# A Fourier filter with a mixture of experts: transform pieces put behind expert steps at an even course, gate and lists in a bank and buffers of their own, float16 from the fourth set on

## The chip, the cores and the metric

The kernel runs on one core of a Trainium2 chip. The metric is device time in microseconds (us), the median over runs. Engines are named as the profile names them: PE (matmuls), PEld (its weight loads), DVE (vector), ACT (scalar), POOL (GpSimd) and SP, which issues most DMAs.

## What is computed

Eight batches of 2496 x 256 numbers are filtered along their length by a Fourier transform, a product and the inverse transform. The 19968 rows that come out go through a mixture of eight experts with noisy top-2 gating:

```python
X = np.fft.rfft(x, axis=1); y = np.fft.irfft(X * F[None], n=S, axis=1).reshape(B * S, D)
noisy = y @ w_gate + np.log1p(np.exp(y @ w_noise)) * noise
top2 = the two largest of each row; w = softmax over them
out[row] += w * (np.maximum(y[row] @ w1[e], 0) @ w2[e])    # for both experts e of the row
```

D is 256, the hidden width F is 1024.

## The kernel before

**Transform.** `fft_stream` writes the filter as a stream of small pieces: `s1` and `kg0` to `kg2` go to the frequencies and multiply, `t3` and `i2` come back, all as matmuls with small tables. Every operand is a sum of a high and a low part, so most products are three matmuls. The first two batches are transformed before any expert runs (`early`); the others stand between expert steps. A batch has two halves of 128 columns, `n` = 0 to 15. When its second half is back, `logit_sum`, `logits` and `gate` choose the experts, `slots` deals out blocks, and `route` makes the lists of rows: one-hot matrices `oc` on DVE, matmuls into `ra` on PE, an indirect add on POOL.

**Experts.** Once a batch is listed, a new *set* of blocks of 512 rows can run: 2, 12, 18, 24, 34, 44, 54, 64 blocks in total after each of the eight sets, then remainders. `expert` yields 13 steps per block: eight for the first product (`hps`, six matmuls of 128x512 each), one, and four for the second (`yps`, 24 matmuls of 128x256 each). ACT applies the relu (`hh`, line 1371), DVE makes the low part (`hl`, line 1372). `_mm3` (lines 123 to 126) writes the three matmuls, so its lines stand for both products and the tiles tell them apart. From set `HALF` on the operands are float16, scaled by powers of two that `wscales` finds (all weights are squared on ACT, `wp`, and the first batches of y are read back); before it they are 32-bit.

**Order.** `run` alternates the two: after each expert step it advances the stream while `PACE` allows, a number of transform steps per set, spread over the set. `pin` keeps rows in the written order on chosen engines; what is not pinned a scheduler orders by its own estimate, and expert steps and transform pieces mix freely there. `self.after(i)` keeps what follows behind instruction `i` on its engine.

**PSUM.** Eight banks: `hps` 2, `yps` 2, `xps` 1, `fps` 3. An expert's third bank is `xps` (line 1353); everything of transform, gate and lists shares `fps`:

```python
tag = self.banks.get(nm, "fps") if self.early else "fps"
third = ("xps", 1) if self.by_dma(ent) else ("yps", 2)
while (state["ready"] < state["i"] + (2 if state["i"] < ALONE else 1)
       and (state["n"] - state["p0"]) * state["len"] <= state["c"] * PACE.get(state["i"], PACES) and step()):
```

Of the kernel before, what the change touches and what calls it, by code (L numbers as in the profile page):

```python
# [24 lines left out]
NG = 22  # L25
# [97 lines left out]
def _mm3(nc, o, lh, ll, rh, rl, start=True, stop=True):  # L123
    nc.tensor.matmul(o, lh, rh, start=start, stop=False)  # L124
    nc.tensor.matmul(o, lh, rl, start=False, stop=False)  # L125
    nc.tensor.matmul(o, ll, rh, start=False, stop=stop)  # L126
# [6 lines left out]
PACE = {0: 110, 1: 200, 2: 60}  # L133
PACES = 115
FILL = {0: 0, 1: 14}
RAW = 3
HALF = 5
# [9 lines left out]
EARLY = {"q1": "hps", "q2": "hps", "q5": "yps", "q6": "yps", "u1": "xps", "u3": "yps"}  # L147
BANKS = {"hps": 2, "yps": 2, "xps": 1, "fps": 3}

MOVES = {0: {"q3": "yps"}, 12: {"q3": "fps"}, 14: {"q3": "yps", "q4": "yps", "q5": "hps", "q6": "hps"}, 26: {"q4": "fps", "q5": "yps", "q6": "yps"}}  # L150


class Moe:
# [40 lines left out]
    def setup(self):  # L194
# [43 lines left out]
        self.xs, self.scaled, self.known, self.owed, self.relu = {}, False, False, [], None  # L238

# [163 lines left out]
    def kg1(self, n, kg):  # L403
# [32 lines left out]
        self.zz[n, kg] = a  # L436

# [85 lines left out]
    def i2(self, n, g0):  # L523
# [12 lines left out]
        w = 128 + E * h  # L536
# [11 lines left out]
        if h:  # L548
            nc.scalar.copy(yt[:, :k, 128:], self.dense[:, g0:g0 + k])
# [122 lines left out]
    def fft_stream(self):  # L672
# [132 lines left out]
        for n in range(2 * FIRSTS, N + 1):  # L805
# [31 lines left out]
            for t in range(tot):  # L837
                while ix < len(X) and ix * tot <= t * len(X):
                    self.pin(X[ix], hold=self.held, only=self.held and [self.nc.tensor.engine])
                    ix += 1  # L840
                    write()
                    yield min(self.done_routes, self.rows)
                while iy < len(Y) and iy * tot <= t * len(Y):
                    if self.held:
                        self.pin(Y[iy], only=[self.nc.tensor.engine])
                    else:
                        Y[iy]()
# [11 lines left out]
    def gate(self, bt, lgp):  # L859
# [12 lines left out]
        nc.scalar.activation(u, lg[:, :, 8:16], AF.Exp)  # L872

# [11 lines left out]
        v.tensor_add(nz, l, lg[:, :, 0:8])  # L885
# [6 lines left out]
        for i in range(2):  # L892
            mi, ci = t(f"m{i}", [RP, NG]), t(f"c{i}", [RP, NG])
# [30 lines left out]
        v.tensor_add(self.dense, self.dense, nz)  # L924
        yield None
# [4 lines left out]

# [6 lines left out]
        v.scalar_tensor_tensor(rw, mm, float(LR - 1), q[:, 8:16], op0=ALU.add, op1=ALU.add)  # L937
# [8 lines left out]
        rb = t("rb", [RP, E])  # L946
        v.tensor_add(rb, q[:RP, 0:8], mm[:RP])
# [23 lines left out]
        v.tensor_add(self.base, self.base, q[:, 8:16])  # L971
        v.tensor_add(self.cnt, self.cnt, q[:E, 16:17])
# [60 lines left out]
    def route(self, bt, hi, lo, row, rf):  # L1033
# [11 lines left out]
        for g0 in range(0, NG, 4):  # L1045
            q = self.ps("ra")[:, :HR]
            for g in range(g0, min(g0 + 4, NG), 2):
                t = P.tile([128, 1024], F16, name="oc", tag=("xh", "xl", "b")[g // 2 % 3], bufs=1)


                ol, vv = t[:RP, 0:4 * LR], t[:RP, 4 * LR:4 * LR + 4 * HR]
                if bt < 2:
                    ol, vv = (a.rearrange("p (l j) -> p l j", j=4) for a in (ol, vv))
                else:
                    ol, vv = (a.rearrange("p (j l) -> p l j", j=4) for a in (ol, vv))

                def w(a):
                    return a if bt < 2 else a.rearrange("p l j -> p j l")

                v.tensor_tensor(w(vv), w(lr[:, :HR]), w(bc(hi[:, g:g + 2], HR)), op=ALU.is_equal)  # L1060
                v.tensor_mul(w(vv), w(vv), w(tv[:, 2 * g:2 * g + 4].unsqueeze(1).to_broadcast([RP, HR, 4])))
                v.tensor_tensor(w(ol), w(lr), w(bc(lo[:, g:g + 2], LR)), op=ALU.is_equal)
                for j in range(4):
                    n = RP if g + j // 2 < NG - 1 else QA
                    nc.tensor.matmul(q, ol[:n, :, j], vv[:n, :, j], start=(g == g0 and j == 0), stop=(j == 3 and g + 2 >= min(g0 + 4, NG)))
# [10 lines left out]
        o = P.tile([HR, LR], F32, name="ro", **(dict(tag="th", bufs=3) if bt < 2 else dict(tag="ut1", bufs=1)))  # L1076
# [257 lines left out]
    def expert(self, parts, may, fill=None):  # L1334
# [5 lines left out]
        while self.ahead:  # L1340
# [12 lines left out]
            third = ("xps", 1) if self.by_dma(ent) else ("yps", 2)  # L1353
            hh = []
            for f in range(8):
# [3 lines left out]
                for kc in range(2):  # L1359
                    wh, wl = w1[f // 2]  # L1360
                    o = (f % 2) * 128
                    _mm3(nc, p, wh[:, kc, o:o + 128], wl[:, kc, o:o + 128], *xT[kc], start=(kc == 0), stop=(kc == 1))
# [24 lines left out]
            for t in range(nt):  # L1387
# [5 lines left out]
                for f in range(8):  # L1393
                    h, l = (a[:, t * 128:(t + 1) * 128] for a in hh[f])
                    hl = w2[f // 2][:, :, f % 2]
                    _mm3(nc, p, h, l, hl[:, 0], hl[:, 1], start=(f == 0), stop=(f == 7))
# [11 lines left out]
    def run(self):  # L1408
# [58 lines left out]
        for _ in self.expert(parts(), may, fill):  # L1467
# [59 lines left out]
```

## Time and profile before

| | us |
|---|---|
| median of 3 runs | 2166.99 |
| lowest, highest run | 2159.28, 2168.4 |
| the profiled execution | 2164.38 |
| its span in the profile | 2162.5 |

Busy times of PE are unions of overlapping matmuls: each is shown with its time through the array, so the distance from one start to the next, not the shown duration, is what one costs. Idle time is shown in brackets behind a row with the engine and tile that ended it. A timeline merges equal neighbours (x4).

### The profile page before, as it was taken

The page shows a single profiled execution, that of the slowest core. Times are in us where ns is not written, and L with a number is a line of the kernel's source. Part 1 is how long each engine was busy: PE and PEld are TensorE (multiplying, and loading weights), DVE is VectorE, ACT ScalarE, POOL GpSimd, SP SyncE. Part 2 cuts the span into 40 slices and gives each one's busy share as a digit, 9 for nine tenths or more (in the row PEclk, how much of TensorE's full clock was granted, in tenths as well). Part 3 has the DMA queues.
Part 4 walks back from the last instruction along what each step waited for, and adds up shares of the span by engine and source line. Part 5 has one row for each costly group of instructions (what it writes and reads, how often), then busy time and mean ns, then how long its engine had stood idle before and what let it go on. Part 6 is the DMA issues. An engine that isn't in the chain of part 4 may idle for free. (4 is left out here: it accounts for less than half of the span.)

```text
span 2162.5 us, 42794 instructions
## 1 busy us (share of the span) xinstructions
PE 2095.9 (97%) x14517; PEld 1595.5 (74%) x14517; DVE 1466.3 (68%) x3221; ACT 1286.1 (59%) x2505; POOL 1029.2 (48%) x946
## 2 busy tenths in 40 slices
PE   8779999999999999999999999999999999999997
PEld 6447988888888888766766676666666666667886
DVE  5866779877978886678665986589666664333443
ACT  6666866786577446656664565555566564333443
POOL 4233334434544344445444453555655665654563
PEclk9989999999999999999999999999999999999999
DMA  9588989999999775767766687666889999869997
GB/s 255 165 259 223 222 223 215 252 228 228 223 214 233 161 156 137 178 150 183 155 156 131 152 182 165 146 121 132 233 210 240 240 249 234 170 142 229 276 280 175
DMA packets 511673, 428.48 MB, mean 198 GB/s; under 512 B 215679, under 2 KB 397015, under 8 KB 511447
## 3 DMA queue, kind: packets, MB, share of 16 engines
q1 hardware_dynamic: 450135, 341.27, 60.2%
q0 software_dynamic: 61312, 84.40, 23.1%
q8 instruction: 116, 1.90, 0.4%
q14 instruction: 110, 0.90, 0.1%
HBM read 263.92 MB, written 122.03 MB: 178 GB/s over the span
## 5 line engine op out<-in xcount | busy, mean ns | idle before, releaser
L1372 DVE SCALAR_TENSOR_TENSOR hl<-hps,hh 128x512 f16<-128x512 f32 (+3 forms) x712 | 432.4, 623 | 356.6 <-ACT hh L1371 354.7
L1399 POOL DMA_INDIRECT out<-stage,ids x316 | 532.9, 1686 | 270.4 <-ACT stage L1398 167.0
L1158 POOL DMA_INDIRECT stage<-y,ids x316 | 347.9, 1101 | 535.7 <-DMA xt<-stage 433.9
L124 PE MATMUL yps<-w,hh 128*128 128x256 f16 (+1 forms) x2048 | 556.5, 278 | 5.2 <-ACT stage L1398 3.4
L125 PE MATMUL yps<-w,hh 128*128 128x256 f16 (+1 forms) x2048 | 551.2, 277 | 0.0
L126 PE MATMUL yps<-w,hl 128*128 128x256 f16 (+1 forms) x2048 | 541.9, 277 | 1.8 <-DVE hl L1372 1.5
L1371 ACT ACTIVATE hh<-hps 128x512 f16<-128x512 f32 (+3 forms) x712 | 376.7, 550 | 198.9 <-PE hps L126 183.8
L125 PE MATMUL hps<-mxl,w1h 128*128 128x512 f16 (+1 forms) x1024 | 394.4, 386 | 2.2 <-DVE mxl L1246 1.3
L126 PE MATMUL hps<-mxh,w1l 128*128 128x512 f16 (+1 forms) x1024 | 394.0, 386 | 0.0
L124 PE MATMUL hps<-mxh,w1h 128*128 128x512 f16 (+1 forms) x1024 | 385.6, 388 | 5.1 <-DVE hl L1372 5.1
L1398 ACT ACTIVATE stage<-yps,gt 128x256 f32<-128x256 f32 x316 | 143.1, 475 | 329.0 <-PE yps L126 202.0
L124 PEld LDWEIGHTS <-hh 128*128 128x128 f16 x1760 | 172.2, 98 | 52.4 <-issue 6.2
L126 PEld LDWEIGHTS <-hl 128*128 128x128 f16 x1760 | 171.5, 98 | 47.9 <-DVE hl L1372 1.9
L125 PEld LDWEIGHTS <-hh 128*128 128x128 f16 x1760 | 172.2, 98 | 34.2 <-issue 2.6
L124 PEld LDWEIGHTS yps<-w,hh 128*128 128x128 f32 x768 | 145.8, 190 | 12.5 <-ACT stage L1398 2.2
L126 PEld LDWEIGHTS yps<-w,hl 128*128 128x128 f32 x768 | 145.0, 190 | 10.3 <-issue 1.7
L125 PEld LDWEIGHTS yps<-w,hh 128*128 128x128 f32 x768 | 145.4, 191 | 4.6
L126 PEld LDWEIGHTS <-w1l 128*128 128x128 f16 x640 | 62.6, 98 | 71.8 <-issue 1.5
L541 ACT COPY yt<-q 117x1024 uint16<-117x1024 uint16 x96 | 90.9, 947 | 40.7 <-PE q L535 32.1
L1228 DVE COPY stage<-xt 128x1024 uint16<-128x1024 uint16 (+2 forms) x174 | 109.0, 679 | 1.4 <-DMA xt<-stage 1.4
L124 PEld LDWEIGHTS <-w1h 128*128 128x128 f16 x640 | 62.4, 98 | 51.5 <-issue 5.5
L125 PEld LDWEIGHTS <-w1h 128*128 128x128 f16 x640 | 62.6, 98 | 51.1 <-issue 3.0
(286 smaller groups left out, 4024.4 us busy)
## 6 DMA issues: line engine op xcount, KB each, us to landing
stage<-w SPq DMA_DIRECT2D x328, 256.0 KB
x<-x SPq DMA_DIRECT2D x88, 256.0 KB
fd<-c SPq DMA_DIRECT2D x77, 240.0 KB
fi<-wpl SPq DMA_DIRECT2D x18, 1024.0 KB
fx<-fd SPq DMA_DIRECT2D x140, 128.0 KB
out<-z SPq DMA_DIRECT2D x24, 702.0 KB
wp<-w SPq DMA_DIRECT2D x64, 256.0 KB
fr<-w SPq DMA_DIRECT2D x16, 1024.0 KB
```

Of the source, the lines that this page charges most:

```text
L124: nc.tensor.matmul(o, lh, rh, start=start, stop=False)
L125: nc.tensor.matmul(o, lh, rl, start=False, stop=False)
L126: nc.tensor.matmul(o, ll, rh, start=False, stop=stop)
L541: e = nc.scalar.copy(yt.bitcast(U16)[:, :k, :256].rearrange("p g (two d) -> p g two d", two=2), p.bitcast(U16)[:RP, :2 * m].rearrange("p ( ...
L1158: self.pin(lambda: nc.gpsimd.indirect_dma_start(out=x.bitcast(I32), out_offset=None, in_=self.y[:BLK + ready * ROWS], in_offset=bass.Indir ...
L1228: nc.vector.tensor_copy(xu.rearrange("p (t two) -> p two t", two=2), ent[3][0][:, 2 * kc:2 * kc + 2, :w])
L1371: self.relu = hold(lambda: nc.scalar.activation(h, p, AF.Relu))
L1372: v = hold(lambda: nc.vector.scalar_tensor_tensor(l, p, 0.0, hf[0], op0=ALU.max, op1=ALU.subtract))
L1398: nc.scalar.activation(o, p, AF.Copy, scale=gate[:, t])
L1399: a = nc.gpsimd.indirect_dma_start(out=self.io["out"][:BLK + ready * ROWS], out_offset=bass.IndirectOffsetOnAxis(ap=ids[:, t:t + 1], axis= ...
```

## The change

1. Pieces of the transform on PE stand behind the last matmul that an expert wrote (`self.mm`), and those on ACT behind the last relu.
2. `COURSE` replaces `PACE`: a line through points (expert steps, transform steps), and the stream may always be one set further ahead.
3. `HALF` goes from 5 to 4: the fourth set runs in float16, its scales are due by step 202 (`READY`) instead of 280.
4. Gate, slots and lists (`APART`) use the bank `xps`; the experts' third bank is `yps` until all lists are done. For batches from the third on, what is read from that bank is copied out (`clean`, `total`, `below`).
5. `route` builds the one-hots of up to two groups (`place`), yields, and then multiplies (`add`); its buffers are `ut0`, `ul`, `ut1` and `gl`.
6. The chosen weights `dense` go to memory in one store per batch in place of a copy into each `yt`.
7. The planes of the tail are prepared from the last filter piece on (`filtered`), not from the last list on.

```diff
-PACE = {0: 110, 1: 200, 2: 60}
-PACES = 115
+COURSE = (0, 55), (100, 172), (178, 268), (256, 365), (386, 462), (516, 554), (646, 640)
-HALF = 5
+HALF = 4
+APART = {"lg", "rk", "sl", "st", "ra"}
+def due(y):
+    for (a, m), (b, n) in zip(COURSE, COURSE[1:]):
+        if y <= b:
+            return m + (n - m) * (y - a) / (b - a)
+    return float("inf")
...
-        tag = self.banks.get(nm, "fps") if self.early else "fps"
+        tag = self.banks.get(nm, "fps") if self.early else "xps" if nm in APART else "fps"
...
+        self.filtered = (n, kg) == (2 * NB - 1, 4)
...
-        w = 128 + E * h
+        w = 128 + (E * h if n < 4 else 0)
-        if h:
+        if h and n < 4:
             nc.scalar.copy(yt[:, :k, 128:], self.dense[:, g0:g0 + k])
...
-                    self.pin(X[ix], hold=self.held, only=self.held and [self.nc.tensor.engine])
+                    with self.after(self.mm), self.after(self.relu):
+                        self.pin(X[ix], hold=self.held, only=self.held and [self.nc.tensor.engine])
...
+        clean = lg[:, :, 0:8]
+        if bt >= 2:
+            clean = P.tile(sh, F32, name="clean", tag="oh1", bufs=1)
+            nc.scalar.copy(clean, lg[:, :, 0:8])
-        v.tensor_add(nz, l, lg[:, :, 0:8])
+        v.tensor_add(nz, l, clean)
...
+        if bt >= 2:
+            y = self.y[BLK + bt * ROWS:BLK + (bt + 1) * ROWS].rearrange("(p g) d -> p g d", p=RP)
+            nc.sync.dma_start(y[:, :, D:], self.dense.bitcast(I32))
...
+            below, total = t("rb", [RP, E]), P.tile([128, E], F32, name="total", tag="gd", bufs=1)
+            v.tensor_copy(total, q[:, 8:16])
+            v.tensor_copy(below, q[:RP, 0:8])
+            v.tensor_add(self.cnt, self.cnt, q[:E, 16:17])
...
+                t = P.tile([128, 4 * LR + 4 * HR], F16, name="oc", tag=("ut0", "ul", "ut1")[made % 3], bufs=1)
...
+                hot = [place(g) for g in gs]
+                yield
+                q = self.ps("ra")[:, :HR]
+                for g, o in zip(gs, hot):
+                    add(q, g0, g, *o)
...
-            third = ("xps", 1) if self.by_dma(ent) else ("yps", 2)
+            third = ("xps", 1) if self.done_routes == NB - 1 else ("yps", 2)
...
-            while (state["ready"] < state["i"] + (2 if state["i"] < ALONE else 1)
-                   and (state["n"] - state["p0"]) * state["len"] <= state["c"] * PACE.get(state["i"], PACES) and step()):
+            while (state["ready"] < state["i"] + 2
+                   and state["n"] <= due(state["y"]) and step()):
-            if state["ready"] >= NB - 1:
+            if self.filtered:
                 state["k"] += 1
```

Two places show how it moves instructions. The first is DVE where it builds the one-hots of the fifth batch's list (lines 1060 to 1062 before, 1089 to 1091 now; 1372 and 1417 are `hl`, 1323 and 1249 a weight split, 546 and 555 the maximum of y). Before:

```order
L1062 TENSOR_TENSOR oc<-half,lo 117x512
L1323 TENSOR_TENSOR w_10592<-stage,w_10592 128x512
L1067 COPY rx<-ra 128x56
L1060 TENSOR_TENSOR oc<-half,hi 117x224
L1062 TENSOR_TENSOR oc<-half,lo 117x512
L1060 TENSOR_TENSOR oc<-half,hi 117x224
L1062 TENSOR_TENSOR oc<-half,lo 117x512
L1323 TENSOR_TENSOR w_10617<-stage,w_10617 128x512
L546 TENSOR_REDUCE ymax<-yt 117x1
L400 TENSOR_TENSOR tl<-fx,th 128x512
L1372 SCALAR_TENSOR_TENSOR hl<-hps,hh 128x512
L1061 TENSOR_TENSOR oc<-oc,half 117x224
```

and now:

```order
L350 TENSOR_TENSOR xl<-x,xh 117x512
L1112 COPY rx<-ra 128x56
L1089 TENSOR_TENSOR oc<-half,hi 117x224
L1091 TENSOR_TENSOR oc<-half,lo 117x512
L438 TENSOR_TENSOR a<-a,b 128x512
L555 TENSOR_REDUCE ymax<-yt 117x1
L1417 SCALAR_TENSOR_TENSOR hl<-hps,hh 128x512
L555 TENSOR_REDUCE ymax<-yt 117x1
L1090 TENSOR_TENSOR oc<-oc,half 117x224
L1249 SCALAR_TENSOR_TENSOR mxl_10136<-stage,xs_8531,mxh_10135 128x512
L1417 SCALAR_TENSOR_TENSOR hl<-hps,hh 128x512
```

Before, three pairs of one-hots (the first begins just above) stand ahead of one `hl`, with weight splits and two transform pieces; now two pairs do, with transform pieces and no weight split, and the multiplication by the row number (1061, now 1090) comes behind the next `hl`.

The second is PE at the first product of the 19th block, the first of the fourth set. Before:

```order
L124 MATMUL hps<-mxh_9845,w1h 128x512
L448 MATMUL q_8017<-cf,a 128x2x64 x4
L533 MATMUL q_8037<-th,hl 117x256
L534 MATMUL q_8037<-tl,hl 117x256
L535 MATMUL q_8037<-th,hl 117x256
L126 MATMUL yps<-w_9807,hl 128x256 x2
L125 MATMUL hps<-mxl_9846,w1h 128x512
L126 MATMUL hps<-mxh_9845,w1l 128x512
L124 MATMUL hps<-mxh_9849,w1h 128x512
L125 MATMUL hps<-mxl_9850,w1h 128x512
L126 MATMUL hps<-mxh_9849,w1l 128x512
```

and now:

```order
L125 LDWEIGHTS w1h
L125 MATMUL hps<-mxl_9743,w1h 128x512
L126 LDWEIGHTS w1l
L126 MATMUL hps<-mxh_9742,w1l 128x512
L124 LDWEIGHTS w1h
L124 MATMUL hps<-mxh_9746,w1h 128x512
L945 MATMUL rk<-rs,small 117x8
L946 MATMUL rk<-rs,small 128x8
L947 MATMUL rk<-small,rs 8x1
L126 MATMUL yps<-w_9696,hl 128x256
L518 MATMUL q_9796<-ident,G 120x128 x4
L126 MATMUL yps<-w_9696,hl 128x256
```

The matmuls of the experts now have weight loads of their own (LDWEIGHTS stands apart for float16 operands), and the gate's three counting matmuls `rk` (lines 945 to 947), of the fifth batch, which came some 15 first-product steps later before, stand here.

## Rows read from the trace of the kernel before

**Rows 1.** The page, part 1: busy us, share of the span, instructions.

```profile
PE 2095.9 (97%) x14517; PEld 1595.5 (74%) x14517; DVE 1466.3 (68%) x3221; ACT 1286.1 (59%) x2505; POOL 1029.2 (48%) x946
```

**Rows 2.** Windows by stage: stretch, length, busy us of each engine, PEclk, DMA share.

```profile
0.00:217.00 217.00, 182.19 (x983) 124.34 (x984) 142.89 (x411) 140.88 (x258) 72.01 (x72) 0.94 0.83 225
217.00:860.00 643.00, 632.09 (x4138) 557.43 (x4138) 512.03 (x1115) 439.01 (x894) 266.89 (x217) 1.00 0.88 208
860.00:900.00 40.00, 36.47 (x229) 28.03 (x228) 27.54 (x47) 27.30 (x49) 17.54 (x20) 1.00 0.81 195
900.00:1530.00 630.00, 626.56 (x4420) 428.93 (x4419) 466.53 (x1067) 373.67 (x682) 316.56 (x275) 1.00 0.69 154
1530.00:2140.00 610.00, 609.50 (x4642) 448.75 (x4640) 312.84 (x567) 300.43 (x610) 351.33 (x361) 1.00 0.96 229
```

**Rows 3.** Waits of PE, 217 to 1566 us: us in total, times, longest.

```profile
PE hps L124 <- DVE hl L1372: 4.7, 6, 1.4
PE yps L124 <- ACT stage L1398: 3.4, 2, 1.8
PE ra L1065 <- DVE oc L1061: 2.2, 3, 1.1
PE yps L126 <- DVE hl L1372: 1.5, 3, 0.7
PE q L411 <- DVE tl L520: 1.4, 1, 1.4
```

**Rows 4.** Timeline of PE, 772 to 776 us: start, us, instruction, idle before.

```profile
773.06 0.28 PE L125 MATMUL yps<-w,hh 128*128 128x256 f32 x1
774.78 0.50 PE L124 MATMUL hps<-mxh,w1h 128*128 128x512 f32 x1 [1.44 <-DVE hl L1372]
```

**Rows 5.** Timeline of DVE, 764 to 777 us.

```profile
767.62 0.68 DVE L1372 SCALAR_TENSOR_TENSOR hl<-hps,hh 128x512 fp32r<-128x512 f32 x1
...
774.05 0.67 DVE L1372 SCALAR_TENSOR_TENSOR hl<-hps,hh 128x512 fp32r<-128x512 f32 x1
```

**Rows 6.** Groups of PE by shape: float32 matmuls of the first kind.

```profile
L124 PE MATMUL hps<-mxh,w1h 128*128 128x512 f32 x384 | 152.5, 402 | 5.1 <-DVE hl L1372 5.1
```

**Rows 7.** Timeline of PE, 300 to 302.5 us, experts in float32.

```profile
299.75 0.37 PE L124 MATMUL yps<-w,hh 128*128 128x256 f32 x1
299.95 0.28 PE L125 MATMUL yps<-w,hh 128*128 128x256 f32 x1
...
300.55 0.39 PE L124 MATMUL hps<-mxh,w1h 128*128 128x512 f32 x1
...
301.94 0.28 PE L124 MATMUL yps<-w,hh 128*128 128x256 f32 x1
```

**Rows 8.** Timeline of PE, 1199 to 1206 us, experts in float16.

```profile
1199.78 0.27 PE L125 MATMUL yps<-w,hh 128*128 128x256 f16 x1
...
1202.95 0.38 PE L124 MATMUL hps<-mxh,w1h 128*128 128x512 f16 x1
...
1204.24 0.27 PE L124 MATMUL yps<-w,hh 128*128 128x256 f16 x1
```

**Rows 9.** Timeline of PE, 1023 to 1026 us, transform behind float16 work.

```profile
1024.70 0.58 PE L533 MATMUL q<-th,hl 120*117 120x512 f32 x1
1025.12 0.39 PE L534 MATMUL q<-tl,hl 120*117 120x512 f32 x1
```

**Rows 10.** Waits of PE, 0 to 217 us.

```profile
PE xps L1238 <- DVE gs L918: 2.7, 1, 2.7
```

**Rows 11.** Tile ra: who waited for it (us, times).

```profile
  DVE rx L1069: 4.8, 4
```

**Rows 12.** Windows for the DMA load (share and GB/s at the end).

```profile
217.00:650.00 433.00, 428.42 (x2810) 378.17 (x2810) 346.86 (x747) 316.33 (x664) 184.65 (x152) 1.00 0.94 226
...
1998.00:2106.00 108.00, 108.00 (x992) 96.82 (x990) 47.34 (x124) 48.26 (x124) 63.61 (x82) 1.00 1.15 274
```

**Rows 13.** Waits of DVE, whole span.

```profile
DVE ymax L620 <- DMA wp<-y: 16.5, 8, 4.5
```

More of the change, by code (lines that the diff above doesn't have):

```diff
@@ L843, in fft_stream @@
                 while iy < len(Y) and iy * tot <= t * len(Y):
[L844 to L847, printed above, removed]
+                    with self.after(self.mm), self.after(self.relu):
+                        if self.held:
+                            self.pin(Y[iy], only=[self.nc.tensor.engine])
+                        else:
+                            Y[iy]()
                     iy += 1
@@ L936, in gate @@
         v.scalar_tensor_tensor(mm, hb, -float(LR), self.base, op0=ALU.mult, op1=ALU.add)
-        v.scalar_tensor_tensor(rw, mm, float(LR - 1), q[:, 8:16], op0=ALU.add, op1=ALU.add)
+        v.scalar_tensor_tensor(rw, mm, float(LR - 1), total, op0=ALU.add, op1=ALU.add)
         v.tensor_single_scalar(rw, rw, 7, op=ALU.arith_shift_right)
@@ L945, in gate @@
         v.scalar_tensor_tensor(mm, beg, float(LR), mm, op0=ALU.mult, op1=ALU.add)
-        rb = t("rb", [RP, E])
-        v.tensor_add(rb, q[:RP, 0:8], mm[:RP])
+        rb = below if bt >= 2 else t("rb", [RP, E])
+        v.tensor_add(rb, below, mm[:RP])
         v.tensor_add(src, src, rb.unsqueeze(1).to_broadcast(sh))
@@ L1044, in route @@
         lr, tv = self.half[:RP, :4 * LR].rearrange("p (l j) -> p l j", j=4), self.half[:RP, 4 * LR:]
-        for g0 in range(0, NG, 4):
[L1046 to L1065, printed above, removed]
@@ new lines, in route, with place, w @@
+        made = 0
+        def place(g):
+            nonlocal made
+            if bt < 2:
+                t = P.tile([128, 1024], F16, name="oc", tag=("xh", "xl", "b")[g // 2 % 3], bufs=1)
+            else:
+                t = P.tile([128, 4 * LR + 4 * HR], F16, name="oc", tag=("ut0", "ul", "ut1")[made % 3], bufs=1)
+                made += 1
+            ol, vv = t[:RP, 0:4 * LR], t[:RP, 4 * LR:4 * LR + 4 * HR]
+            if bt < 2:
+                ol, vv = (a.rearrange("p (l j) -> p l j", j=4) for a in (ol, vv))
+            else:
+                ol, vv = (a.rearrange("p (j l) -> p l j", j=4) for a in (ol, vv))
+            def w(a):
+                return a if bt < 2 else a.rearrange("p l j -> p j l")
+            v.tensor_tensor(w(vv), w(lr[:, :HR]), w(bc(hi[:, g:g + 2], HR)), op=ALU.is_equal)
+            v.tensor_mul(w(vv), w(vv), w(tv[:, 2 * g:2 * g + 4].unsqueeze(1).to_broadcast([RP, HR, 4])))
+            v.tensor_tensor(w(ol), w(lr), w(bc(lo[:, g:g + 2], LR)), op=ALU.is_equal)
+            return ol, vv
@@ new lines, in add @@
+        def add(q, g0, g, ol, vv):
+            for j in range(4):
+                n = RP if g + j // 2 < NG - 1 else QA
+                nc.tensor.matmul(q, ol[:n, :, j], vv[:n, :, j], start=(g == g0 and j == 0), stop=(j == 3 and g + 2 >= min(g0 + 4, NG)))
+        for g0 in range(0, NG, 4):
+            gs = range(g0, min(g0 + 4, NG), 2)
+            if bt < 2:
+                q = self.ps("ra")[:, :HR]
+                for g in gs:
+                    add(q, g0, g, *place(g))
+            else:
+                hot = [place(g) for g in gs]
+                yield
+                q = self.ps("ra")[:, :HR]
+                for g, o in zip(gs, hot):
+                    add(q, g0, g, *o)
```

18 lines of the change are left out of this document (11 added, 7 removed).

## The prediction

> **What bounds the kernel now.** I read the engines' shares first. TensorE (PE) is busy 97% of the span and the next engine, VectorE (DVE), 68% [rows 1]. The table by stage says where the other 3% is. From 0 to 217 us PE is busy 182.19 of 217 us. From 217 to 2140 us it idles 10.91, 3.53, 3.44 and 0.50 us, 18.4 us in all, at the full clock (2.4 GHz, column PEclk 1.00; the first stage shows 0.94) [rows 2]. So only two things can shorten the long middle: fewer nanoseconds per matmul, or fewer of those 18.4 us. DMA, POOL and the other engines matter only through PE's waits.
>
> The list of waits between 217 and 1566 us names them: PE waits for `hl`, for the stage copy of ScalarE (ACT), for the one-hot pieces `oc`, for `mxl`, none over 1.8 us long [rows 3]. One of them seen closely: PE should start the next matmul at about 773.18 and starts it at 774.78 with 1.44 us of idle, until `hl` is there [rows 4]. So a wait costs some 0.16 us more than its idle time, since the array drains. That view has 22 waits in eleven lines, of which the five costliest stand here, so the middle loses 18.4 + 22 x 0.16 = 22 us. On DVE, two `hl` start at 767.62 and 774.05, and between them stand one-hot pieces, weight splits and transform pieces, 5.7 us of work that is not `hl` [rows 5]: such a burst is what makes `hl` late.
>
> **The change, part by part.**
>
> *Float16 one set earlier.* 384 float32 matmuls of the first kind, 16 to a block, make 24 blocks in float32 now [rows 6]. `HALF` 4 moves the set of `PAIRS[3]` = 3 pairs, 6 blocks of 512 rows, to float16. The price is the distance between starts, since busy times overlap. In float32, five matmuls of 256 columns take from 299.95 to 300.55, 0.120 us each, and six of 512 columns from 300.55 to 301.94, 0.232 each [rows 7]. In float16, 29 of 256 columns take from 1199.78 to 1202.95, 0.109 each, and six of 512 from 1202.95 to 1204.24, 0.215 each [rows 8]. A block has 48 of the wide and 96 of the narrow: 48 x 0.017 + 96 x 0.011 = 1.9 us, for 6 blocks 11 us. PE is never the one waited out here, so all of it lies on the path. Float32 now and then also shows 0.20 in place of 0.12 (299.75 to 299.95, [rows 7]); at some five such steps a block, an estimate, that is 0.4 us, 2.4 us for six blocks.
>
> Against that, a float32 transform piece behind float16 work starts slowly: L533 to L534 takes 0.42 us instead of 0.23 [rows 9], others some 0.1. About 30 such groups move into float16 surroundings by the order: 30 x 0.1 = 3 us lost. Net: 11 + 2.4 - 3 = 10.4 us gained; ends 7 (no slow steps saved, 0.13 lost each) and 14 (no loss).
>
> The Trainium skill, TensorE: Matmul & The Clock Gate, in "Step-by-step: what each phase is for", holds that a matmul's time is its number of columns and nothing else. By it float32 and float16 of one width cost the same, this term is nil and the sum below ends at 2153; the rows at either width disagree by 8 to 10%, and the measurement decides.
>
> *Pieces behind expert steps, one even course.* No matmul of the transform is added or taken away; three tiny ones of one more scale come, under 0.5 us. Until now the transform ran at 110 steps per set, then 200, 60 and 115. Now it advances about 1.2 steps per expert step to the 256th, and 0.7 after that, and each batch is ready some 56 expert steps, over four blocks, ahead of its set. What it can win is the waits. The order shows it working on DVE: the batch that makes the burst of rows 5 now has two pairs of one-hots and no weight split ahead of the `hl`, and builds them a step before PE takes them. The waits for `oc` (2.2 us) should go, those for `hl`, `tl`, `mxl` (10.2 us of idle with their smaller kinds) should shrink, those for ACT shrink less. I take half of 22, 11 us. The ends are 0 (they move) and 20 (nearly all go); nothing excludes new ones, so below nothing I allow 10 us of loss.
>
> *Own bank.* `lg`, `rk`, `sl`, `st` and `ra` leave the transform's three banks for the single `xps`. Per batch that is 11 groups of matmuls, some 72 over six batches, each able to wait for the reader of the one before. PE's nearest rows: one wait in this very bank for the gate's DVE chain took 2.7 us [rows 10], and DVE waited for `ra` 4.8 us over four times [rows 11]. I price it at nothing, since `clean`, `below` and `total` are copied out at once and the pieces lie steps apart; upper end see the rival. The expert's third bank becomes `yps`: its next user comes two or more steps after the last reader, no cost.
>
> *Scaling earlier.* All weight squares must be done by expert step 202 instead of 280. By the order the 64th stands before the 96th `hh` rather than the 129th. 64 loads of 256 KB (16.8 MB) were spread over some 460 us, 37 GB/s, and now take 87 expert steps in place of 120: 14 GB/s more. This stretch runs at 226 GB/s; the late one moved 274 with PE busy without a gap [rows 12]. So it is hidden; if that cover were gone, ACT would get its weights late. The twelve `wp` loads of y do make DVE wait, 16.5 us in eight waits [rows 13]; they stay, only earlier.
>
> *Small pieces.* ACT loses the 36 copies of `dense` and gains 6 of `clean`, DVE gains some 20 tiny operations, POOL a scale and a gate product in set four, SP six scattered stores of `dense`. SP waits for that add with weight loads queued behind; they run ahead of use, as its present waits do without PE showing them. The tail's planes start earlier (at the last filter step); the tail waits for nothing now [rows 2], so this gives nothing. The first 217 us keep the order of PE row for row and their 35 us of idle.
>
> **Sum.** 2164.4 us (profiled execution) - 10.4 - 11 = 2143. The median of the runs, 2167.0, lies 2.6 above that execution, and the runs spread from 2159 to 2168; I put the forecast at 2145.
>
> **The rivals.**
>
> *The waits only move.* DVE has the same work, and the even course gives it gates and routes at once with the weight splits. For it: DVE's longest pieces are unchanged. Against: the order has fewer long stretches between two `hl` for the PE work beside them. Time: 2164.4 - 10.4 = 2154, with the median's offset up to 2157.
>
> *The single bank becomes a chain.* PE is in order; if a `ra` or `st` stands before the reader of the last has run, all expert matmuls behind it wait. At the 2.7 us of rows 10, three waits a batch are 18 x 2.7 = 49 us, and none of the 11 us is won: 2164.4 - 10.4 + 49 = 2203. It turns slower than before at 4 waits (10.4 / 2.7) if nothing else is won, at 8 if my 11 us hold, and slower by 0.5% at 8 and 12. Against it: the copies out of the bank, and steps between groups in the order.
>
> *Columns alone set the time.* The float16 set wins nothing, only the waits: 2164.4 - 11 = 2153. This is the rule of the Trainium skill, TensorE: Matmul & The Clock Gate, named above. The rows speak plainly against it.
>
> *Weights come late.* The denser scaling and the faster transform before step 178 fill the DMA queues; at one wait of 1.8 us [rows 3] in each of 8 blocks, 14 us are lost of the 21: 2158.
>
> **How the numbers follow.** Forecast 0.69 (own range 2128 to 2152), waits only move 0.18, chain 0.05, columns alone 0.03, late weights 0.05. The bounds of the terms: best 2164.4 - 14 - 20 = 2130, with the runs' spread of 4 us 2126; worst kept case, waits move and some come new, 2164.4 - 7 + 7 = 2164. Range 2126 to 2164. 0.5% of 2167 is 10.8 us, about what a measurement of this kernel can tell from no change, so faster begins below 2156. Most of the forecast's 0.69, half of "waits move" and of "columns alone" lie there: 0.76. Within 0.5%: 0.19. Slower: 0.05, the chain.
>
> **What would show it.** Right: float32 rows x288 in place of x384 [rows 6]; starts 0.109 and 0.215 us apart in the set before the present change-over; no wait for `oc`, and a PE idle between 217 and 2140 us of 6 to 13 us instead of 18.4; the same 35 us in the first stage. Wrong: waits of `ra`, `rk` or `st` on DVE readers with over 1 us each (chain); the same 18 us under other names (moved); ACT or PE waiting for `stage<-w` (late weights); equal starts in both types (columns).

## The result, and the profile after

The changed kernel takes 2190.05 us (median of 4 runs, 2185.44 to 2192.36), the kernel before 2167.69 (median of 4, 2159.28 to 2169.16): a ratio of 1.0108, 95% interval 1.0082 to 1.0134. It is slower by 1.1%, where the prediction said faster by 1%. The profiled execution of the change took 2190.24 us, its span is 2188.5 us.

The page's first part and the windows by stage, the same stretches as [rows 1, 2] (length, busy us of PE, PEld, DVE, ACT, POOL; then PEclk, DMA share, GB/s):

```profile
PE 2100.7 (96%) x14522; PEld 1565.8 (72%) x14522; DVE 1464.5 (67%) x3243; ACT 1285.7 (59%) x2475; POOL 1035.2 (47%) x955
```

```profile
0.00:217.00 217.00, 181.50 (x997) 125.28 (x998) 144.61 (x413) 143.89 (x267) 71.61 (x72) 0.95 0.81 228
217.00:860.00 643.00, 620.91 (x4032) 521.10 (x4033) 512.48 (x1141) 444.42 (x878) 269.70 (x217) 0.98 0.84 208
860.00:1566.00 706.00, 689.44 (x4808) 468.85 (x4807) 512.30 (x1141) 412.02 (x740) 349.05 (x308) 0.99 0.73 165
```

The first stage is as it was. From 217 to 860 us PE now idles 22 us in place of 11, from 860 to 1566 us 17 in place of 7, and PEclk, 1.00 in both stretches before, is 0.98 and 0.99: some of the busy time too is slow.

To see where the time went I gave every matmul its **usual distance** to the next start (the 40th percentile over all matmuls of its line and shape in the same trace). The sum of these is the **floor**, and what a stretch takes beyond them I call **lost**: waits of PE and matmuls slower than usual. Before: floor 2029 us, lost 61 in the first stage, 28 from 217 to 860, 24 from 860 to 1566, 2 later. After: floor 2021, lost 60, 51, 37 and 3. The floor fell by 8 us, as float16 should make it; the losses rose by 35. Of the losses after 217 us, 13 us are matmuls that run at 1.2 GHz; before, that clock shows after 217 us only at the very end.

The longest wait of PE between 217 and 860 us, in the timelines of DVE and of PE (start, us, instruction, idle before it and what ended it) and in windows around it:

```profile
556.68 1.22 DVE L629 TENSOR_REDUCE ymax<-wp 117x1 f32<-117x1024 bf16 x1 [7.59 <-DMA wp<-y]
...
558.26 0.68 DVE L1417 SCALAR_TENSOR_TENSOR hl<-hps,hh 128x512 fp32r<-128x512 f32 x1
```

```profile
554.35 0.40 PE L125 MATMUL hps<-mxl,w1h 128*128 128x512 f32 x1
554.58 0.39 PE L126 MATMUL hps<-mxh,w1l 128*128 128x512 f32 x1
558.99 0.50 PE L124 MATMUL hps<-mxh,w1h 128*128 128x512 f32 x1 [4.02 <-DVE hl L1417]
...
560.55 0.63 PE L126 MATMUL hps<-mxh,w1l 128*128 128x512 f32 x1
560.97 0.63 PE L124 MATMUL hps<-mxh,w1h 128*128 128x512 f32 x1
```

```profile
550.00:554.60 4.60, 4.60 (x32) 3.97 (x30) 0.00 (x0) 3.99 (x8) 3.58 (x3) 1.00 0.90 247
554.60:558.80 4.20, 0.37 (x2) 0.00 (x0) 2.12 (x5) 1.14 (x3) 3.73 (x5) 1.00 1.17 241
...
560.00:563.40 3.40, 3.40 (x9) 2.62 (x9) 3.40 (x11) 0.60 (x1) 0.00 (x0) 0.51 0.93 230
```

A read-back of y for the scales is late, at a DMA share of 1.17. DVE waits 7.59 us for it, the expert's `hl` stands behind it in DVE's order, PE stands still for 4.02 us. About a microsecond after PE is back, the clock is at its lower level (0.51, which is 1.2 GHz): float32 matmuls of 512 columns start 0.42 us apart (560.55 to 560.97) where they did 0.23 (554.35 to 554.58). So the gap is paid, and then about eight matmuls more at 0.2 us each.

The same in the second stretch, in the timelines of SP's queue and of ACT, with the windows around it:

```profile
1264.39 0.41 SPq L634 DMA_DIRECT2D fr<-w  x1
1358.28 0.39 SPq L634 DMA_DIRECT2D fr<-w  x1
```

```profile
1353.76 1.08 ACT L1443 ACTIVATE stage<-yps,gt 128x256 f32<-128x256 f32 x2 [0.93 <-issue]
1364.86 2.56 ACT L640 ACTIVATE fi<-fr,wtab 128x512 f16<-128x512 f32 x4 [10.02 <-DMA fr<-w]
1367.32 0.45 ACT L1443 ACTIVATE stage<-yps,gt 128x256 f32<-128x256 f32 x1
```

```profile
1350.00:1360.00 10.00, 10.00 (x82) 7.89 (x81) 4.52 (x8) 3.72 (x7) 1.25 (x2) 1.00 0.70 143
1360.00:1370.00 10.00, 6.63 (x42) 4.48 (x42) 3.96 (x7) 5.14 (x10) 8.10 (x7) 0.94 1.00 340
1370.00:1380.00 10.00, 6.29 (x29) 3.11 (x28) 8.69 (x15) 9.12 (x17) 3.94 (x4) 0.84 1.10 351
1380.00:1390.00 10.00, 10.00 (x47) 6.19 (x47) 9.66 (x17) 7.56 (x13) 0.52 (x1) 0.70 1.18 326
```

The tail's planes now start at the last filter step. The first is split without trouble at 1270 us. The second is loaded into the buffer `fr`, which DVE's filter product reads until 1352.95 us (L436, 1352.26 and 0.69 long); SP issues the load at 1358.28, when ACT has its split next in order, so that ACT waits 10.02 us with an output copy of the expert behind it. The loads that follow drive the DMA share to 1.18. From 1350 to 1404 us 13.6 us are lost, 3.6 before.

Lastly the waits, of PE, ACT and DVE between 217 and 1566 us (us in total, times, longest); PE's answer to [rows 3], the last to [rows 13]:

```profile
PE hps L124 <- DVE hl L1417: 6.9, 6, 4.0
PE yps L126 <- DVE hl L1417: 5.7, 7, 2.5
PE q L353 <- ACT xh L349: 5.7, 3, 2.1
PE yps L124 <- ACT hh L1416: 4.4, 5, 1.7
PE yps L124 <- ACT stage L1443: 3.6, 3, 2.0
PE hps L124 <- ACT stage L1443: 3.4, 1, 3.4
PE yps L124 <- DVE hl L1417: 3.3, 2, 2.0
```

PE's waits for `hl` grew from 6.2 to 15.9 us, and those for pieces and copies that ACT makes (`xh`, `hh`, `stage`, `yt`) from 5.1 to 19.7. ACT's waits for loads, before and now:

```profile
ACT w1h L1322 <- DMA stage<-w: 18.1, 16, 2.3
...
ACT wp L603 <- DMA wp<-w: 5.9, 3, 4.1
```

```profile
ACT w1h L1367 <- DMA stage<-w: 17.9, 14, 3.0
...
ACT wp L612 <- DMA wp<-w: 14.4, 8, 3.6
...
ACT fi L640 <- DMA fr<-w: 12.6, 3, 10.0
```

```profile
DVE ymax L629 <- DMA wp<-y: 12.6, 3, 7.6
```

ACT's wait for the weights of the squares grew from 5.9 to 14.4 us, the one for the experts' own weights did not (18.1 and 17.9), and the one for `fr` is new. The read-backs wait less in all than before, but in three waits up to 7.6 us instead of eight up to 4.5.

### The profile page after: what moved, and what is told of

Read it like the earlier page. It is cut to its first block, busy times and chain, and to the rows that moved or that the text cites. A ratio compares the mean times of both kernels' runs of the same rounds, so it can differ in the third digit from the quotient of the medians.

```text
span 2188.5 us, 42807 instructions
## 1 busy us (share of the span) xinstructions
PE 2100.7 (96%) x14522; PEld 1565.8 (72%) x14522; DVE 1464.5 (67%) x3243; ACT 1285.7 (59%) x2475; POOL 1035.2 (47%) x955
## 4 chain that ended last, share of the span: by engine, by line
PE 59%; DVE 3%; DMA 2%; ACT 1%; issue 1%; SPq 0%; POOL 0%; POOLq 0%; DVEq 0%; ACTq 0%
PE yps L124 9%; PE yps L126 9%; PE yps L125 9%; PE hps L124 9%; PE hps L125 9%; PE hps L126 9%; PE q L457 1%; DMA fr<-w 1%; DVE hl L1417 1%; PE q L518 1%; PE u L470 0%; DMA out<-stage,ids 0%; DMA y<-yt 0%; DMA fi<-wpl 0%; PE q L544 0%
## 5 line engine op out<-in xcount | busy, mean ns | idle before, releaser
L126 PE MATMUL yps<-w,hl 128*128 128x256 f16 (+1 forms) x2048 | 550.0, 278 | 5.8 <-DVE hl L1417 5.7
L124 PEld LDWEIGHTS <-hh 128*128 128x128 f16 x1952 | 191.1, 98 | 53.0 <-issue 4.6
L126 PEld LDWEIGHTS <-hl 128*128 128x128 f16 x1952 | 190.9, 98 | 49.8 <-issue 4.0
L125 PEld LDWEIGHTS <-hh 128*128 128x128 f16 x1952 | 191.2, 98 | 38.8 <-issue 4.6
L126 PEld LDWEIGHTS <-w1l 128*128 128x128 f16 x736 | 72.3, 98 | 85.5 <-issue 3.5
L124 PEld LDWEIGHTS yps<-w,hh 128*128 128x128 f32 x576 | 111.9, 194 | 14.8 <-ACT stage L1443 5.4
L124 PEld LDWEIGHTS <-w1h 128*128 128x128 f16 x736 | 72.3, 98 | 65.4 <-issue 11.6
L125 PEld LDWEIGHTS <-w1h 128*128 128x128 f16 x736 | 72.3, 98 | 65.2 <-issue 8.6
L126 PEld LDWEIGHTS yps<-w,hl 128*128 128x128 f32 x576 | 111.5, 195 | 9.1 <-DVE hl L1417 4.9
L1249 DVE SCALAR_TENSOR_TENSOR w1l<-stage,sc,w1h 128x512 f16<-128x512 f32 x92 | 68.5, 745 | 71.6 <-ACT w1h L1248 70.8
L125 PEld LDWEIGHTS yps<-w,hh 128*128 128x128 f32 x576 | 112.0, 195 | 3.1 <-issue 0.6
L1153 POOL CAST ids<-lt 128x4 int32<-128x4 f32 (+3 forms) x66 | 28.3, 429 | 170.4 <-DMA lt<-lst 169.8
```

Source lines behind the costliest of these rows:

```text
L126: return nc.tensor.matmul(o, ll, rh, start=False, stop=stop)
L1153: nc.gpsimd.tensor_copy(ids, t)
L1249: self.nc.vector.scalar_tensor_tensor(l, x, s, h, op0=ALU.mult, op1=ALU.subtract)
```

## The experiments

All were run in at least three rounds beside the kernel before. Ratio with its interval, then from the profiled execution the floor, the losses (us) from 217 to 860 us, what of that falls before 540 us, and the losses from 860 to 1566 us, and how often the clock fell to 1.2 GHz between 217 us and the kernel's last matmuls.

| run | ratio | floor | lost 217-860 | of it to 540 | lost 860-1566 | half clock |
|---|---|---|---|---|---|---|
| before | 1 | 2029 | 28 | 11 | 24 | 0 |
| the change | 1.0108 (1.0082-1.0134) | 2021 | 51 | 26 | 37 | 8 |
| e1_after_half5 | 1.0201 (1.0156-1.0246) | 2029 | 51 | 25 | 44 | 7 |
| e2_before_half4 | 1.0170 (1.0129-1.0211) | 2024 | 79 | 22 | 22 | 5 |
| e3_after_pace | 1.0120 (1.0085-1.0156) | 2024 | 50 | 28 | 44 | 5 |
| e4_after_free | 1.0053 (1.0030-1.0076) | 2022 | 46 | 26 | 31 | 2 |
| f1_after_late | 1.0082 (1.0065-1.0099) | 2024 | 60 | 29 | 26 | 7 |
| f2_after_noread | 1.0136 (1.0105-1.0167) | 2021 | 47 | 28 | 45 | 8 |
| f3_after_free_late | 1.0040 (1.0021-1.0058) | 2022 | 51 | 27 | 28 | 4 |
| f4_before_held | 0.9993 (0.9977-1.0008) | 2029 | 32 | 11 | 24 | 2 |
| g4_after_noscale | 1.0060 (1.0040-1.0079) | 2022 | 29 | 17 | 44 | 4 |
| g2_after_half5_pace_late | 1.0058 (1.0038-1.0077) | 2029 | 45 | 27 | 27 | 4 |
| g5_free_late_early16 | 1.0076 (1.0046-1.0105) | 2025 | 49 | 27 | 25 | 3 |
| e5_after_shared | 1.0056 (1.0034-1.0077) | 2024 | 46 | 19 | 32 | 6 |
| h1_before_shifted | 0.9999 (0.9982-1.0016) | 2029 | 31 | 11 | 29 | 2 |
| h2_after_dense_with_rows | 1.0109 (1.0070-1.0149) | 2025 | 47 | 23 | 44 | 7 |
| h4_before_dense_store | 0.9990 (0.9969-1.0010) | 2029 | 30 | 11 | 26 | 2 |
| h3_four_undone | 1.0011 (0.9990-1.0031) | 2021 | 52 | 21 | 20 | 5 |
| k1_four_noscale | 0.9861 (0.9838-0.9884) | 2019 | 18 | 9 | 16 | 0 |
| k2_four_early_spread | 1.0075 (1.0053-1.0097) | 2021 | 48 | 17 | 16 | 5 |

How far one trace can be trusted: the change and f1_after_late issue the same matmuls in the same order up to 1392 us, and lost 51 and 60 us between 217 and 860. A difference of 10 us between single traces is no finding there; the ratios are. The profiled executions of f1 and f3 are also 7 and 9 us slower than the medians of their runs. The stretch from 217 to 540 us varies less: the kernel before and its variants f4, h1 and h4 lose 11 us in it, the change and f1 26 and 29.

**First set: which part?** Theories: the packed scaling work, the course with pieces held behind expert steps, the single bank.

```diff
 e1: in the change
-HALF = 4
+HALF = 5
```

> The changed kernel with HALF back at 5, so that the fourth set is float32 again and the scales are due by step 280 instead of 202. Theory S (the packed scaling work makes the new waits before 860 us, some 22 us, half of them the half clock that follows a wait): 2190 - 22 + 10 for the lost float16 set = about 2178, no wait for a read-back of y over 5 us, and no half clock before 860 us but one. Theory C (the course and the pieces behind expert steps make them): 2190 + 10 = about 2200, with the same half clocks. Theory B (the single bank): also about 2200.

```diff
 e2: in the kernel before
-HALF = 5
+HALF = 4
```

> The kernel before with HALF at 4 alone. Theory S: the scaling is as packed as in the changed kernel, so the 10 us of the float16 set are won and some 22 us of waits come: about 2179, with half clocks before 700 us. Theories C and B: 2167 - 10 = about 2157, PE's idle time between 217 and 860 us near the 11 us of the kernel before.

```diff
 e3: in the change, the pace rule of before
-                   and state["n"] <= due(state["y"]) and step()):
+                   and (state["n"] - state["p0"]) * state["len"] <= state["c"] * PACE.get(state["i"], PACES) and step()):
```

> The changed kernel with the old PACE rule in place of the course. Theory S: 2185 to 2195, the scaling is as packed. Theory C: most of the 35 us of new lost time goes, about 2160, and the waits of 1350 to 1512 us go with it. Theory B: 2185 to 2195, and waits of ra, rk or st remain.

```diff
 e4: in the change, twice
-with self.after(self.mm), self.after(self.relu):
+if True:
```

> The changed kernel with its pieces no longer held behind the last expert matmul and the last relu (both issue orders taken away); course, bank and float16 set stay. Theory C in the form that the holding makes pieces late: about 2165, and the waits of PE for the high part of x (line 353) go. Theory S and theory B: 2185 to 2195.

The fourth set back in float32 makes the change slower by some 0.9%, so float16 there is a gain, and the scaling alone is not the fault; why by more than the 8 us of the floor is open. Float16 alone in the kernel before costs 1.7%: its set then meets a batch that is not ready, with PE waiting 9.81 us for the gate's `rs` (the timeline of e2):

```profile
761.00 0.56 PE L927 MATMUL rk<-rs,small 117*117 117x8 f32 x2 [9.81 <-DVE rs L911]
```

That set begins only at 773 us. From 217 to 540 us the packed scaling is all that e2's edit changes, ACT waits 17.8 us for its loads, and 22 us are lost where the kernel before loses 11: packing does cost there. But it is not what the change loses in that stretch by itself. In e1 the squares are spread again, to 662 us, ACT does not wait for them after 217 us, and the stretch still loses 25 us, against 26 in the change. The old pace changes nothing. Pieces not held give back 0.55%.

**Second set: the planes, the read-backs, the holding alone.**

```diff
 f1: in the change
-            if self.filtered:
+            if state["ready"] >= NB - 1:
```

> The change with one part undone: the planes of the tail are started, as before the change, only when the last batch is ready, and not at the last filter step. Theory T (the early planes cost): the wait of ACT for the filter table's load, 10 us, and the slow stretch at about 1350 to 1404 us, 13.6 us above the usual distances of matmuls, go with their half clock: 0.5 to 0.7% faster than the change, 1.004 to 1.006 of the kernel before. Theory D (every new order of the pieces brings its own losses, and where they fall is chance): some of it comes back elsewhere, 1.007 to 1.012.

```diff
 f2: in the change
-        yield from pairs(load_y, top_y, len(Y))
+        for _ in range(len(Y) + 2):
+            yield
```

> The change without the twelve read-backs of y for the scales (loads and reductions; the scale of the first float16 set then rests on the later batches alone): on VectorE nothing waits for that load any more with hl queued behind it. Theory R (the read-backs, moved into a stretch with less slack, cost): the gap at 555 us and the ones after it to 630 us go, 51 us lost between 217 and 860 us become some 40, 0.4 to 0.5% faster than the change, 1.005 to 1.007 of the kernel before. Theory D: 1.009 to 1.012, the gaps come at other places of the same stretch.

f3 has the edits of e4 and f1 together:

> Two parts undone at once: pieces not held behind the last expert step, and the planes of the tail started as before. The holding alone cost 0.5%. Theory T: the two add up, 12 us and 10 to 13 us less than the change, 0.998 to 1.001 of the kernel before. Theory D: the planes were no longer in the way once the pieces were free (that run had a longest gap of 5 us), so as without the holding alone, 1.004 to 1.007.

```diff
 f4: in the kernel before, around both kinds of pieces, self.mm set by the expert's _mm3
+with self.after(self.mm), self.after(self.relu):
```

> The kernel before with one part of the change alone: each transform piece is held behind the last expert matmul and the last relu issued. Theory H (holding costs by itself, as pieces can no longer fill a gap ahead of their place and all of a piece's engines get them late): 1.004 to 1.008. Rival: holding costs only with the early scaling work and the new course, since that is what makes the engines full: 0.998 to 1.002.

The late planes remove their stretch. The window from 1350 to 1404 us, first the change, then f1:

```profile
1350.00:1404.00 54.00, 46.92 (x319) 32.49 (x320) 31.85 (x51) 31.88 (x57) 23.41 (x22) 0.91 0.97 281
```

```profile
1350.00:1404.00 54.00, 54.00 (x390) 38.26 (x391) 32.49 (x52) 32.66 (x58) 26.12 (x26) 1.00 0.80 182
```

In time they give 0.26%, about half of what the trace promised, with intervals that overlap, so their price in time is not shown by this run alone. Leaving out the read-backs, the very wait shown above, gives nothing: the loss of 8.7 us from 600 to 650 us fell to 0.5, but as much appeared elsewhere. My theory of that one wait fell. Holding alone costs nothing in the kernel before, though its removal helps in the change: it costs only together with something else in the change, and with what is not shown.

**Third set: all of the scaling work, the rest of the edits, the bank.**

```diff
 g4: in the change; f2's edit, and
-                nc.sync.dma_start(t, io["w1" if i < 4 * E else "w2"][i // 4 % E, i % 4])
-                nc.scalar.activation(t, t, AF.Square, accum_out=self.wquart[:, i % 4:i % 4 + 1])
-                v.tensor_reduce(self.wmax[:, i // 4:i // 4 + 1], self.wquart, axis=AX.X, op=ALU.max)
+                v.memset(self.wmax[:, i // 4:i // 4 + 1], 0.25)
```

> The change without the scaling work of the weights and of y (64 loads of 256 KB with their squares on ScalarE, 12 read-backs of y with their reductions on VectorE): the scales rest on a constant and on the later batches alone. Theory L (this work, packed into 202 expert steps, comes on top of a DMA share that was already 0.91 to 1.00 there; ScalarE then waits 14 us for wp with relu and output copies behind it): the loss between 217 and 860 us falls from 51 to about 30 us, that at 1350 to 1404 us stays, 0.998 to 1.003 of the kernel before. Rival E (the gate and list edits and the new order cost by themselves): 1.006 to 1.011.

g2 has the edits of e1, e3 and f1 together:

> The change with its fourth set in float32 again (and the scaling spread as before), with the old pace of the transform and the planes of the tail started as before: what is left of the change is the own bank, the gate and list edits and the holding. Theory L (these are neutral; the load on DMA and ScalarE by the denser work is what costs): 0.998 to 1.003. Rival E (they cost by themselves, which is why the runs with one of the other parts undone were no better): 1.007 to 1.015.

```diff
 g5: the edits of e4 and f1, and in the first stage, a slot each
+            if 6 <= t < 22:
+                next(self.preps)
-            while not self.scaled and state["due"] * READY < NPREP * state["y"]:
+            while not self.scaled and state["due"] * READY < (NPREP - 16) * state["y"]:
```

> The change with pieces not held and the tail's planes late (1.004 when alone together), and 16 of the 64 weight squares moved ahead of the first expert step, where the DMA share was 0.66 to 0.75 at 60 to 120 us: the rest then stands as far apart as in the kernel before. Theory L: 0.998 to 1.002. Rival: the first stage, where PE waits on ScalarE, becomes longer by as much as is won later (16 x 0.64 = 10 us of ScalarE): 1.003 to 1.008.

```diff
 e5: in the change
-        tag = self.banks.get(nm, "fps") if self.early else "xps" if nm in APART else "fps"
+        tag = self.banks.get(nm, "fps") if self.early else "fps"
-            third = ("xps", 1) if self.done_routes == NB - 1 else ("yps", 2)
+            third = ("xps", 1) if self.by_dma(ent) else ("yps", 2)
```

> The change with the bank part undone: lg, rk, sl, st and ra share the three banks of the transform again, and the expert's third bank alternates as before. Theory L: the own bank is neutral (its waits on the page are 2.4 us in all), 1.008 to 1.013. Rival B: the own bank is what delays the gates and routes, 1.000 to 1.006.

Without the scaling work the loss between 217 and 860 us falls from 51 to 29, as the theory had it, and the time by only 0.5%: 860 to 1566 us lost 44. The shared banks give back 0.5%, which rival B had and I had not; no wait on a reader of the bank is longer than 1.4 us in the change, so why they do is not shown. g2 lay between the two theories, and says more than that: with the fourth set in float32, the scaling spread (ACT waits 4.2 us for `wp`), the old pace and the late planes it is still 0.6% slower than the kernel before, and loses 27 us from 217 to 540 us. So the bank, the gate and list edits, the holding and the store of `dense` cost that much without the denser scaling; the holding (f4) and the store (h4, below) cost nothing by themselves. Moving squares ahead gave nothing.

**Fourth set: chance or sum?** Every part undone gave a little. Either the parts add up, or any other order of the pieces costs about as much.

```diff
 h1: in the kernel before
-PACE = {0: 110, 1: 200, 2: 60}
-PACES = 115
+PACE = {0: 113, 1: 200, 2: 60}
+PACES = 118
```

> The kernel before with no part of the change: only its pace is shifted by 3 steps per set (110 to 113, 115 to 118), so that the same pieces fall between other expert steps. Theory D (any other order of the same work loses, since gaps of a few us and the half clock after them fall by chance, and before stands in an order that had none): 1.004 to 1.012. Rival L (only the added or packed work costs): 0.998 to 1.002.

```diff
 h2: in the change (h4: the reverse, in the kernel before)
-        w = 128 + (E * h if n < 4 else 0)
+        w = 128 + E * h
-        if h and n < 4:
+        if h:
-            nc.sync.dma_start(y[:, :, D:], self.dense.bitcast(I32))
```

> The change with dense again copied by ScalarE into the rows of y and stored with them, in place of six stores of their own with 2574 packets of 32 bytes each. Theory P (those stores hold up the DMA engines with the weights queued behind: 137 GB/s in the 5 us after the first of them where it was 250 to 330 around it): 0.3 to 0.6% faster than the change, 1.005 to 1.008. Rival (36 copies on ScalarE take back what the DMA engines win): 1.009 to 1.013.

> The kernel before with this one part of the change: dense stored by itself, six times 2574 packets of 32 bytes, and not copied into the rows of y. Theory P: 1.003 to 1.006. Rival (hidden): 0.998 to 1.002.

h3 has the edits of e4, f1, e5 and h2 together:

> The change with four parts undone that each stood at 0 to 0.5%: pieces not held, tail planes late, shared banks, dense stored with the rows. What is left is float16 a set earlier with its denser scaling, the even course, and the rest of the gate and list edits. If the parts add up, 1.0108 less 0.0055, 0.0026, 0.0052 and some 0.004 of the store: 0.992 to 0.997. Theory D (each of them only brought another order, and none adds up): 1.003 to 1.008.

A shifted pace costs nothing: chance in the order is out as the sole cause, as far as this order and those of f4 and h4, which cost nothing either, can tell. The scattered stores cost nothing either, in both kernels. And the four parts together give back 0.97%, where alone they gave 0.55, 0.26, 0.52 and 0 (1.3%): within the intervals they add up, though to less than I expected. What is lost from 860 to 1566 us is 20 us now, where the change lost 37 and the kernel before 24.

**Last set: what still hides the gain.** k1 is h3 with the edit of g4; k2 is h3 with 24 preparations in the first stage, as in g5, and `READY` 8 steps later.

> The four parts undone as in the run before (1.001), and the scaling work of the weights and of y left out as well (64 loads with their squares, 12 read-backs; the scales rest on a constant and on the later batches). Theory L (what still hides the gain of float16 is the packed scaling work: 52 us lost between 217 and 860 us in place of 28): that loss falls to 30 us, the total to 0.989 to 0.993 of the kernel before. Rival (the even course and the remaining edits lose it, whatever the scaling does): 0.997 to 1.001.

> The four parts undone, and the scaling work kept but spread: 24 of the 64 weight squares ahead of the first expert step, the rest over 210 steps in place of 202, so that they stand about as far apart as in the kernel before. Theory L: about half of the 22 us of excess loss goes, 0.994 to 0.999, faster than both kernels. Rival (16 of them moved ahead gave nothing, as the first expert steps then lost 2 to 3 us more and the read-backs of y stay): 1.000 to 1.004.

The windows from 217 to 860 us, of h3 and of k1:

```profile
217.00:860.00 643.00, 619.39 (x4033) 517.21 (x4032) 507.80 (x1124) 434.94 (x879) 264.13 (x217) 0.98 0.84 205
```

```profile
217.00:860.00 643.00, 640.71 (x4257) 535.06 (x4256) 519.64 (x1143) 430.63 (x815) 276.99 (x234) 1.00 0.81 190
```

PE's idle falls from 23.6 to 2.3 us, its clock stays at 1.00, and the span from 2172.5 to 2131.6. So the scaling work, 64 loads of 256 KB with squares of 0.63 us each and 12 read-backs, is worth 1.5% here, three times what it was worth with the other parts in place. That is the price of the work itself, which the kernel before does too, not of packing it. ACT's waits for weights, in h3 and in k1 (217 to 1566 us):

```profile
ACT w1h L1364 <- DMA stage<-w: 21.7, 13, 3.9
ACT wp L612 <- DMA wp<-w: 20.5, 9, 4.1
```

```profile
ACT w1h L1360 <- DMA stage<-w: 29.3, 19, 3.7
```

The wait for the experts' own weights is longer in k1, and harms nothing; the 20.5 us of `wp` are gone. A version that keeps the work and loses its cost was not found. k2 waits for `wp` only 0.9 us, but pays in the first stage, where PE's busy time, 181.50 us in the change, drops in k2 to

```profile
0.00:217.00 217.00, 173.66 (x922) 115.04 (x923) 130.51 (x401) 146.45 (x288) 66.03 (x65) 0.92 0.81 234
```

so that the first stage loses 73 us in place of 60, and it still loses 48 us from 217 to 860. So the late squares are not all of it. Whether the loads, the squares or the read-backs weigh most was not separated in the version with the four parts undone, nor was the kernel before run without its scaling, so how much of k1's 1.4% is owed to the change is open. The best version that computes everything, h3, is level with the kernel before.

## Why the prediction was wrong

The step that failed is the gain of the pieces behind expert steps on one even course, with the prices of nothing for the bank and the tail's planes. The sum took 11 us off; instead the trace lost 35 us more, in new waits of PE for `hl` and for ACT and in the clock behind them. Four parts undone together (h3: holding, tail planes, own bank, store of `dense`) give back 0.97% of the 1.08%, 21 us. What they do to each other is shown in time only; for the bank no wait explains it.

**Float16 one set earlier: right.** 288 float32 matmuls of the first kind are left of 384 [rows 6]:

```profile
L124 PE MATMUL hps<-mxh,w1h 128*128 128x512 f32 x288 | 117.2, 409 | 5.9 <-DVE hl L1417 5.8
```

The floor fell by 8 us, forecast 10.4 (7 to 14); the floors of all runs with that set in float16 lie 4 to 10 us below 2029. By the rule of the Trainium skill, TensorE: Matmul & The Clock Gate, "Step-by-step: what each phase is for", that only columns count, the floor would have stayed; it fell in the change, and came back to 2029 in e1 and g2, which undo the set. One reading in the term was wrong. The 0.42 us of [rows 9] are no slow start: the float16 matmul ahead begins only 0.02 us earlier,

```profile
1024.68 0.38 PE L126 MATMUL hps<-mxh,w1l 128*128 128x512 f16 x1
```

and from there to 1025.12 the two take 0.44 us, their usual 0.215 and 0.23. The 3 us that I took off for such places had no ground in these rows.

**"I take half of 22, 11 us": wrong, and the sign.** PE's waits between 217 and 2140 us did not shrink from 18.4 us of idle to the forecast 6 to 13, they grew to 39 (22.1, 0, 16.6 and 0.5 in the four stretches of [rows 2]), and with the half clock the losses grew by 35 us. I had allowed 10 below nothing, and then put only 7 into the upper end of the range. Of the waits that I looked at, those for `oc` went (2.2 to 0 us from 217 us on), but those for `hl`, which were to shrink, grew from 6.2 to 15.9, and those for ACT, from 5.1 to 19.7, grew most. I read a list of old waits for what the course could win, and not the engines' queues for what it would put in their place. The old pace in the change (e3) gives nothing back, so the course neither won nor lost anything that can be told from no change; the holding, which I had not priced apart from it, is worth 0.55% in the change and nothing alone.

**"I price it at nothing" of the bank.** The chain of the rival does not show: no wait of a `ra` or `st` of over 1.4 us. Yet undoing the bank part gave 0.5%. The rival's mechanism is not seen, its sign is; this stays open.

**"So this gives nothing" of the tail's planes: wrong.** I looked at the tail, which had no wait to lose, and not at the load's buffer. In the change 13.6 us are lost around the second split, in f1 1.5 us in the same stretch; in the whole time f1 gains 0.26%, less than the two intervals can tell apart.

**"So it is hidden": wrong, but it does not explain the change by itself.** I compared GB/s: 14 more on 226, where the late stretch moved 274 [rows 12]. All 64 squares ran between 171 and 537 us where they had taken from 176 to 630, and ACT's wait for them rose from 5.9 to 14.4 us. I wrote that if the cover were gone "ACT would get its weights late": it did, but the squares' weights alone, not the experts'. e2 shows a price, 11 us in the kernel before. In the change it cannot be read off, since e1 and g2, with the squares spread, lose as much from 217 to 540 us. g4 and k1 price the work as a whole at 0.5 and 1.5%. The rival "weights come late" is near this, but its sign, a longer wait for `stage<-w`, did not come; its 14 us, at a chance of 0.05, would not have reached the measured time either. The DMA engines' busy share does not tell more than GB/s: from 217 to 540 us it was 0.96 before and is 0.91 in the change, and the late stretch of [rows 12] shows 1.15 with PE busy throughout.

**"They stay, only earlier": half right.** The read-backs of y did stay and waited less in sum, but in three waits, one of 7.59 us; in a trace that one costs PE 4.0 us and the clock. Leaving them out alone won nothing, however.

**What I had not in the sum at all** is the clock. In [rows 2] it is 1.00 from 217 us on, so I took the busy time of a matmul as given, and each new wait at its idle plus 0.16 us.

## What to carry to other kernels

Where a change packs work into a stretch, ask what stands in order behind its first waiting instruction: here neither the GB/s of the DMA engines nor their busy share told. Price a gap of a few microseconds on PE at its length and the slow matmuls behind it. Undo suspected parts together as well as one by one: here each alone gave 0 to 0.55%, four gave 1%, and the same piece of work was worth 0.5% with the other parts in place and 1.5% without them. And try a part both ways, alone in the old kernel and taken out of the new one: the packed scaling cost 11 us in the one and nothing that shows in the other.

## What the hardware showed

TensorE's clock fell to 1.2 GHz (0.51 granted from 560.00 to 563.40 us) shortly after PE had stood still for 4.02 us and was busy again, and 3.4 us later it was back at its upper level. Each of its eight falls in the change came about 1 to 2 us after a wait of PE of 1.4 to 4.0 us, but not each such wait was followed by one: after 2.13 us at 372.6 us the clock stayed up. In k1, whose longest PE wait between 217 and 1566 us is 1.9 us, it never fell in that stretch. The Trainium skill, TensorE: Matmul & The Clock Gate, "HAM oscillation — how this bites in real kernels", describes this for waits on DMA between groups of matmuls: the slow clock is paid beyond the wait. The trace agrees, 13 us of it in the change, and here the wait reaches PE through DVE and ACT.

Six stores of 2574 packets of 32 bytes each changed nothing in the time, as h4 shows by itself (0.9990), though GB/s fell to 137 in the 5 us after the first one in the change. The Trainium skill, DMA: Bandwidth & Descriptors, "Specifications", wants at least 512 bytes for full rate; the rate was low in those 5 us, and the time shows no cost.
